# A planner in the kernel orders all operations of attention and two MLPs; joined attention tails, half-bank score tiles, 576-column elementwise work

## The chip, the core and the metric

The kernel runs on one core of one Trainium2 chip. The metric is device time in microseconds. The core has TensorE (PE, matmuls, with PEld for its weight loads), VectorE (DVE), ScalarE (ACT), GpSimd (POOL) and SyncE (SP), which issues the DMA transfers here.

## What is computed

```python
# 4 batches, 8 heads, 576 positions, 64 columns a head
scores = scale * np.matmul(q, k.transpose(0, 1, 3, 2))
mask = (rel >= 0) & (rel < 128)
scores = np.where(mask, scores + bias[None], -1000000000.0)
attn = np.exp(scores - np.max(scores, axis=-1, keepdims=True))
attn = attn / (np.sum(attn, axis=-1, keepdims=True) + 1e-09)
x = np.matmul(attn, v)                       # then (4, 576, 512)
h = np.maximum(x @ w_in, 0.0)                # first MLP, 1024 wide
gate = 1.0 / (1.0 + np.exp(-conv_out))       # conv_out: 3 taps along positions
x = h * gate @ w_out
h = gelu(x @ w2_in); u, v = split(h)         # second MLP
v_n = (v - mu) / np.sqrt(var + 1e-06) * g_ln
v_s = np.einsum('ts,bsd->btd', w_sg, v_n) + b_sg[None, :, None]
out = x + (u * v_s) @ w2_out
```

## The kernel before

Two heads of a batch make a pair, so there are 16 pairs, four a batch. A pair's scores are nine row tiles (qk_rt, L288): for each head four of 128 queries, and one that holds the last 64 queries of both heads. A row tile sees at most 256 keys, since the window is 128. VectorE adds the bias and takes the maximum (sm_max, L323), ScalarE takes the exponential and its sum (sm_exp, L340), TensorE transposes the result (tr1, tr2, L364 and L373) and multiplies it with V.

Precision is kept by splitting a number into a high and a low part that TensorE takes fast: a product is then three fast ones (high by high, high by low, low by high). Pairs 0 to 2 (NAT = 3) take native fp32 scores instead, from 64 rows of a head each. The other 13 pairs split each head (ld_head, hi_head, lo_head, L220 to L262): load, copy of the high part on ScalarE, two differences over 64 rows on VectorE, two transfers that put the parts beside each other. For pairs 0 to 5 the product with V is native fp32 (av, L397); for the other ten it is split too (ev_h, ev_l, av_a), and P is scaled by the reciprocal sums before it is transposed (sm_norm, L355). The last 64 queries of the two heads are four products of 64 columns or rows (L416, L417, or L485, L486).

The first MLP works on half a batch: 290 columns (a column of its neighbour on either side) by eight tiles of 128. For each: 12 products (m1, L593), relu, three taps (m1_c0, m1_c12, L615 and L627), tanh, gate (m1_g2, L635), split (m1_gh, m1_gl). The second product (m2, L649) of one half runs between the first products of the next. Its result goes to DRAM (x2d) and comes back for the second MLP, with V tiles (vt, L771), U tiles (ut, L844), the product with w_sg (m4, L861) and the last product (m5, L897). Weights come as 64-bit numbers and are converted by ScalarE, VectorE and GpSimd (split64, L180).

The order is written by hand. at(t, fn) puts a function in a list under a time t; the list is sorted by t and called, and each engine gets its instructions in that order (with what the framework moves). Times come from constants such as the spacing of the pairs, TP = 10.813 in the first batch. To keep TensorE occupied in the first batch, warm (L531) multiplies the identity by itself, and nothing reads the result: 14 times at first (WM0), once beside each row tile of pairs 0 to 3 (WMP).

```python
    T0 = TP
    for p in range(B * NP):
        T = TP if p < NP else TQ if p < 2 * NP else TS
        att_pair(p, a, T, T0)
        a, T0 = a + T, T
    START = 4 * TP + ST0
```

## Time and profile before

| | us |
|---|---|
| runs (median of 3) | 615.26 (615.2 to 615.96) |
| profiled execution, span of its instructions | 613.6 |
| runs' median above that span | 1.7 |
| PE busy | 591.6 (96%) |
| PEld busy | 546.9 (89%) |
| DVE busy | 467.9 (76%) |
| ACT busy | 384.2 (63%) |
| POOL busy | 183.4 (30%) |

The profile gives its execution's span; no time of its own around the span is given, so the comparison with the runs is by their median. A busy time is the union of the times of an engine's instructions. Matmuls are pipelined: each is shown for some 0.3 us, while the next one starts after 0.1 to 0.2, so a busy TensorE need not be at its full rate, and what a matmul costs is read from the start of the next one.

### The profile page before, as it was taken

What the parts mean: (1) busy time and instruction counts of PE and PEld (TensorE: products, weight loads), DVE (VectorE), ACT (ScalarE), POOL (GpSimd) and SP (SyncE); (2) the same over time, 40 slices, a digit from 0 to 9 for tenths busy, and PEclk for the clock granted to TensorE, in tenths of its full rate; (3) what the DMA queues carried; (4) which work ended last, traced back from release to release, by engine and by line L of the source; (5) the groups of instructions that cost most, each with busy time, mean ns of one, the idle gap of its engine ahead of it and who ended that gap; (6) DMA issues with size and microseconds to landing.
All of it is one profiled execution on the core that took longest, in us unless ns stands there. A gap on an engine that the chain in (4) does not pass through costs nothing.

```text
span 613.6 us, 11909 instructions
## 1 busy us (share of the span) xinstructions
PE 591.6 (96%) x4148; PEld 546.9 (89%) x4148; DVE 467.9 (76%) x1195; ACT 384.2 (63%) x1034; POOL 183.4 (30%) x258
## 2 busy tenths in 40 slices
PE   7999998999999999999999979999999999999997
PEld 5778987888798999999999969988999999999997
DVE  4777899999999999999857899769856547527522
ACT  4566777778787878887756666567545335526320
POOL 3440355543332233323222131621312311131030
PEclk9999998999999999999999989999999999999999
DMA  7443544432333334321004453352222211102132
GB/s 247 167 129 105 168 136 121 110 98 78 96 81 89 104 97 116 90 64 44 21 19 139 150 154 97 112 151 84 67 77 76 81 49 59 50 19 60 40 88 77
DMA packets 43040, 58.44 MB, mean 95 GB/s; under 512 B 6626, under 2 KB 28130, under 8 KB 42980
## 3 DMA queue, kind: packets, MB, share of 16 engines
q1 hardware_dynamic: 42980, 57.69, 32.1%
q8 instruction: 32, 0.52, 0.3%
q14 instruction: 28, 0.23, 0.1%
HBM read 40.56 MB, written 9.44 MB: 81 GB/s over the span
## 4 chain that ended last, share of the span: by engine, by line
PE 69%; DVE 20%; issue 4%; ACT 3%; DMA 3%; POOL 0%; SPq 0%; DVEq 0%; ACTq 0%
PE m2p L664 8%; PE m5p L904 8%; PE m1p L604 8%; PE ups L851 8%; PE vps L778 7%; PE m4p L868 3%; PE m4p L870 3%; PE m4p L869 3%; PE warm L534 3%; DVE c L629 2%; PE S L304 2%; PE A L475 2%; PE S L315 2%; DVE ws L171 2%; DVE c L630 2%
## 5 line engine op out<-in xcount | busy, mean ns | idle before, releaser
L604 PE MATMUL m1p<-x,w 128*128 128x290 f32 x768 | 127.6, 306 | 1.0 <-ACT h L611 1.0
L664 PE MATMUL m2p<-g,wo 128*128 128x288 f32 x768 | 118.8, 299 | 6.0 <-ACT g L104 3.0
L664 PEld LDWEIGHTS m2p<-g,wo 128*128 128x128 f32 x768 | 107.0, 190 | 7.9 <-ACT g L104 3.5
L604 PEld LDWEIGHTS m1p<-x,w 128*128 128x128 f32 x768 | 110.3, 193 | 3.9 <-ACT h L611 1.8
L346 ACT ACTIVATE P<-t,mx 128x256 f32<-128x256 f32 (+1 forms) x144 | 68.0, 473 | 16.5 <-DVE mx L337 8.5
L647 POOL TENSOR_TENSOR g<-c,g 128x288 fp32r<-128x288 f32 x48 | 42.8, 892 | 71.7 <-ACT g L104 70.8
L337 DVE CUSTOM_DVE_ANT_0 t<-S,bias_t 128x256 f32<-128x256 f32 (+1 forms) x128 | 48.2, 380 | 12.2 <-PE S L304 5.8
L904 PE MATMUL m5p<-gg,w 128*128 128x288 f32 x384 | 54.5, 294 | 0.0
L904 PEld LDWEIGHTS m5p<-gg,w 128*128 128x128 f32 x384 | 52.5, 188 | 0.6
L851 PE MATMUL ups<-x,w2h 128*128 128x288 f32 x256 | 51.7, 295 | 0.0
L887 POOL TENSOR_TENSOR gg<-u,gg 128x288 fp32r<-128x288 f32 x32 | 26.0, 815 | 62.8 <-ACT gg L883 62.8
L629 DVE SCALAR_TENSOR_TENSOR c<-h,cw,c 128x288 f32<-128x288 f32 x64 | 36.4, 569 | 10.3 <-ACT c L621 10.3
L633 ACT ACTIVATE c<-c 128x288 f32<-128x288 f32 x64 | 28.2, 441 | 23.7 <-DVE c L630 23.5
L815 POOL TENSOR_TENSOR mv<-mv,mhalf 128x1 f32<-128x1 f32 x18 | 16.2, 900 | 89.3 <-DVE mv L814 89.3
L851 PEld LDWEIGHTS ups<-x,w2h 128*128 128x128 f32 x256 | 41.4, 188 | 0.7 <-DVE u L858 0.2
L315 PE MATMUL S<-qkt 128*128 128x256 f32 x130 | 40.6, 320 | 1.2 <-DVE mx L337 1.1
L778 PE MATMUL vps<-w2h,x 128*128 128x512 f32 x128 | 40.9, 396 | 0.9 <-DVE zv L801 0.6
L883 ACT ACTIVATE gg<-u 128x288 fp32r<-128x288 f32 x32 | 14.1, 443 | 40.4 <-DVE u L877 40.4
L868 PE MATMUL m4p<-ws,vn 128*128 128x288 f32 x128 | 37.9, 296 | 0.0
L851 PE MATMUL ups<-x,w2l 128*128 128x288 f32 x128 | 37.8, 295 | 0.0
L869 PE MATMUL m4p<-ws,vn 128*128 128x288 f32 x128 | 37.7, 294 | 0.0
L870 PE MATMUL m4p<-ws,vn 128*128 128x288 f32 x128 | 37.7, 294 | 0.0
(179 smaller groups left out, 1504.4 us busy)
## 6 DMA issues: line engine op xcount, KB each, us to landing
wr<-in_w_in_dram SPq DMA_DIRECT2D x16, 512.0 KB, 3.8
st<-in_qk_dram SPq DMA_DIRECT2D x26, 288.0 KB, 2.9
qkt<-qkt SPq DMA_DIRECT2D x52, 144.0 KB, 2.4
x2d<-x2o SPq DMA_DIRECT2D x32, 144.0 KB, 2.2
st<-x2d SPq DMA_DIRECT2D x16, 288.0 KB, 2.8
vr<-in_v_dram SPq DMA_DIRECT2D x16, 256.0 KB, 3.0
wr<-in_w_out_dram SPq DMA_DIRECT2D x16, 256.0 KB, 2.7
res<-x2d SPq DMA_DIRECT2D x24, 144.0 KB, 2.1
```

The lines of the kernel that those rows point to most:

```text
L315: pe.matmul(ps, T[:, c:c + 128], T[:, 704 + k0:704 + k0 + 256], start=j == 0, stop=j == n - 1)
L337: dve.tensor_tensor_reduce(t[:, 0:w], src, bs, -0.125, 3e38, ALU.add, ALU.min, mx)
L346: act.activation(P[:, 0:w], t[:, 0:w], AF.Exp, bias=mx[:, i:i + 1], scale=-1.0, accum_out=sm[:, i:i + 1])
L604: pe.matmul(ps, W1[k][w][:, ms], x[:, xi, :], start=n == 0, stop=n == 11)
L629: dve.scalar_tensor_tensor(c, h[:, 1:HS + 1], cw[:, 1, m:m + 1], c, ALU.mult, ALU.add)
L664: pe.matmul(ps, WO[m][:, w, cs], g[:, gi, :], start=(m == 0 and j == 0), stop=(m == 7 and j == 2))
L778: pe.matmul(ps, X[:, xi, k, ts], E[w][:, k, 512:1024], start=j == 0, stop=j == 11)
L851: pe.matmul(ps, E[w][:, k, d * 128:d * 128 + 128], X[:, xi, k, hf * HS:hf * HS + HS], start=j == 0, stop=j == 11)
L868: pe.matmul(ps, vn[:, 0, ds], ws[k][:, 0, cs], start=k == 0, stop=False)
L869: pe.matmul(ps, vn[:, 0, ds], ws[k][:, 1, cs], start=False, stop=False)
L870: pe.matmul(ps, vn[:, 1, ds], ws[k][:, 0, cs], start=False, stop=False)
L904: pe.matmul(ps, E["w3"][k][:, w, c * 128:c * 128 + 128], g[:, gi, :], start=j == 0, stop=j == 11)
```

## The change

The kernel is rewritten. A class Plan takes every operation with its engine, a cost from a formula, a due time t, the data that it reads and writes and the buffers that it needs. run() places them one after the other: on each engine the operation with the earliest due time among those that could start, else the one that could start first, with buffers given out in the order of their first due time. The instructions are then issued in the order so found, and the framework moves none (manual_schedule). Parts of the computation change with it:

- native scores for 4 pairs (NAT = 4), over 128 rows, half of them zeros; 8 pairs with the native product with V and 8 with the split one (APATH) instead of 6 and 10
- a head is split by one difference over 128 rows, and three transfers, each into the place that the one before has read
- the tails of two heads are one 128x128 product (L600, L601; L710, L711)
- four score tiles of 256 columns lie in two PSUM banks; before, two tiles
- in the split pairs the result, not P, is scaled: the reciprocals are spread to 640 columns, transposed and multiplied in
- the MLP's products take 288 columns a half, and its elementwise work (taps, tanh, gate, split) takes both halves at once, 576 columns; all eight m1 tiles of a batch stand ahead of its m2 products by due time
- no warm products

```diff
-NAT, NTM, AM = 3, 7, 'bbbbbbaaaa'
-TP, TQ, TS = 10.813, 10.095, 15.399
...
-WM0, WMP = 14, [1, 1, 1, 1]
+APATH = (7, 9, 10, 11, 12, 13, 14, 15)
...
+NL, LDH, PH, PB0, ALEAD, D0, DS = 28, 15.079, 83.144, 39.047, 10.405, 0.5, 1.939
...
+class Plan:
...
+            for e in ENG:
+                best = None
+                for o in ready[e]:
+                    s = max(free[e], o["r"], free["POOL"] if o["x"] else lock if e == "POOL" else 0.0)
+                    k = (0, o["t"], o["i"]) if s <= free[e] + 1e-6 else (s, o["t"], o["i"])
...
+        for o in order:
+            o["fn"]()
...
+def us_dve(n, ptr=0, fast=0):
+    return (130 + n / 1.92 if fast else 70 + n / 0.96 + 60 * ptr) / 1000
...
+    ctx.enter_context(tc.manual_schedule())
...
+    tag("mm", 2, tiles=bank[0:2])
+    tag("S", 4, tiles=[bank[2 + i // 2][:, 256 * (i % 2):256 * (i % 2) + 256] for i in range(4)])
+    tag("T", 2, tiles=bank[4:6])
...
+    def head(g, t):
...
+        op_copy(HHI, t - LDH + 4, lambda: r(K.ap()), st.ap, (st,), ((K, 0),), S)
+        op_sub(HLO[g % len(HLO)], t - LDH + 4.7, lambda: r(A.ap()[:, 64:640]), st.ap,
+               K.ap, (st, (K, 0)) + ZA, ((A, 0),), S)
+        load(t - LDH + 5.5, lambda: L.ap()[64:128], lambda: A.ap()[64:128, 64:640], ((A, 0),) + ZL, ((L, 0),), 147456)
+        load(t - LDH + 6, lambda: A.ap()[64:128, 64:640], lambda: K.ap()[0:64], ((K, 0), (L, 0)), ((A, 0),), 147456)
+        load(t - LDH + 6.5, lambda: K.ap()[0:64], lambda: K.ap()[64:128], ((A, 0),), ((K, 0),), 147456)
...
+            def tail():
+                o = Bk.ap()[:, 0:128]
+                pe.matmul(o, PT[0, 1].ap()[:, 384:512], vb()[:, 3, :], start=True, stop=False)
+                pe.matmul(o, PT[1, 1].ap()[:, 384:512], vb()[:, 4, :], start=False, stop=True)
...
+        for k in (1, 2):
+            opx("DVE", us_dve(S, 1), t + 0.4 + 0.7 * k, lambda k=k: dve.scalar_tensor_tensor(
+                c.ap(), h.ap()[:, k:k + S], cw[:, k, m:m + 1], c.ap(), ALU.mult, ALU.add), hh + ("cw",), (c,))
```

TensorE at the program's start, before (nat holds the native queries and keys; S is a score tile, T a transpose, warm the product that nothing reads):

```order
L304 MATMUL S<-nat 128x128
L304 MATMUL S<-nat 128x256
L534 MATMUL warm<-ident 128x128 x16
L304 MATMUL S<-nat 128x256
L534 MATMUL warm<-ident 128x128
L368 MATMUL T_238<-ident,P 128x128
L534 MATMUL warm<-ident 128x128
L307 MATMUL S<-nat 64x192
```

And with the change, with the semaphores waited for (ps_74 and ps_75 are the two banks of scores, kn and qn native keys and queries):

```order
L504 MATMUL ps_74<-kn,qn 128x128 [waits DMAHW1_49,DMAHW0_49,DVE_49]
L504 MATMUL ps_74<-kn,qn 128x256
L504 MATMUL ps_75<-kn,qn 128x256 x2
L504 MATMUL ps_74<-kn,qn 128x192 [waits DVE_49]
L504 MATMUL ps_74<-kn,qn 128x192 [waits DMAHW2_49,Pool_49]
L504 MATMUL ps_74<-kn,qn 128x128
L504 MATMUL ps_75<-kn,qn 128x256 [waits DVE_49]
L504 MATMUL ps_75<-kn,qn 128x256
```

The reads of these tiles on VectorE with the change:

```order
L527 ISA t,sm<-ps_74,bias_t 128x128 [waits DVE_49,PE_49]
L527 ISA sm 128x1
L527 ISA t,sm<-ps_74,bias_t 128x256
L527 ISA sm 128x1
L527 ISA t,sm<-ps_75,bias_t 128x256 [waits PE_49]
L527 ISA sm 128x1
L527 ISA t,sm<-ps_75,bias_t 128x256 [waits Activation_49]
```

The warm products are gone, five row tiles stand at the head of the queue, and VectorE waits for TensorE once for each bank, not for each tile.

TensorE in the middle of the first MLP, before (m1p and m2p are results of its first and second products, A of the split product with V):

```order
L604 MATMUL m1p<-x,w_93 128x290 x2
L604 MATMUL m1p<-x,w_94 128x290
L315 MATMUL S<-qkt 128x256
L317 MATMUL S<-kl,qkt 128x256
L315 MATMUL S<-qkt 128x256
L317 MATMUL S<-kl,qkt 128x256
L664 MATMUL m2p<-g,wo_99 128x288 x3
L664 MATMUL m2p<-g,wo_100 128x288 x3
```

And with the change, at the end of the first batch's first products (ps_72 and ps_73 are the two banks of the MLP; L778 is the first product, L808 the second, L509 a split score, L565 a transpose, L590 a product with V):

```order
L778 MATMUL ps_73<-x,w_766 128x288 x12
L626 MATMUL ps_79<-ident_80,xt 128x128
L778 MATMUL ps_72<-x,w_842 128x288 x12
L778 MATMUL ps_73<-x,w_842 128x288 x12
L808 MATMUL ps_72<-g,wo 128x288 x12
L565 MATMUL ps_76<-ident_80,P 128x128 x4
L808 MATMUL ps_73<-g,wo 128x288 x6
L590 MATMUL ps_78<-v_98,pt 128x64 x3
L808 MATMUL ps_73<-g,wo 128x288 x6
L509 MATMUL ps_75<-kh,qa_94 128x192
```

First and second products no longer alternate: the last first product is followed at once by the second products, and the attention's pieces stand between runs of six or twelve.

SP's queue in the first MLP batch with the change (kl, qa and kh are the three operands of a head, raw is a weight, v a load of V; before, a head had two such transfers, qkt<-qkt):

```order
L319 DMA kl_96<-qa_94 64x576 [waits DMAHW2_49,PE_49]
L319 DMA raw<-in_w_out_dram 128x1024 [waits DMAHW3_49]
L319 DMA qa_94<-kh 64x576 [waits DMAHW4_49,DMAHW2_49]
L319 DMA kh<-kh 64x576 [waits DMAHW5_49,DMAHW4_49]
L319 DMA raw<-in_w_out_dram 128x1024 [waits DMAHW6_49,DVE_49]
L319 DMA v_99<-in_v_dram 128x4x128 [waits DMAHW7_49,PE_49]
```

A transfer of a head now waits in SP for the landing of the head's transfer before it, with weight and V loads behind it.

## Rows read from the trace of the kernel before

**Rows 1.** By stage: us; busy PE, PEld, DVE, ACT, POOL; clock; DMA share; GB/s.
```profile
0.00:59.70 59.70, 55.39 (x347) 42.84 (x347) 40.22 (x131) 35.47 (x108) 20.03 (x41) 1.00 0.50 162
59.70:225.00 165.30, 156.67 (x1133) 141.40 (x1132) 156.83 (x440) 129.69 (x390) 64.81 (x94) 0.99 0.39 108
225.00:330.00 105.00, 104.99 (x800) 100.46 (x799) 86.68 (x242) 79.75 (x236) 31.16 (x50) 1.00 0.23 65
330.00:401.70 71.70, 67.33 (x469) 65.39 (x468) 62.54 (x112) 45.60 (x102) 21.31 (x20) 0.98 0.44 133
401.70:613.60 211.90, 207.23 (x1408) 196.79 (x1407) 121.65 (x273) 93.64 (x201) 46.09 (x53) 1.00 0.23 68
```

**Rows 2.** Timeline of TensorE: start, us, instruction; first matmuls and first MLP product.
```profile
4.31 1.62 PE L304 MATMUL S<-nat 64*128 64x128 f32 x4 [4.31 <-DMA nat<-in_qk_n_dram]
5.86 6.23 PE L534 MATMUL warm<-ident 128*128 128x128 f32 x32
...
59.68 0.38 PE L604 MATMUL m1p<-x,w 128*128 128x290 f32 x1
```

**Rows 3.** Chain of waits, two runs of 12 MLP products.
```profile
212.26 1.63 PE m1p L604 x12
...
220.35 1.60 PE m2p L664 x12
```

**Rows 4.** Timeline of TensorE: native score, product with V, transpose, split score.
```profile
20.49 0.70 PE L304 MATMUL S<-nat 64*128 64x256 f32 x2
21.11 0.32 PE L408 MATMUL O<-vr,pt 128*128 128x64 f32 x1
...
31.24 0.27 PE L368 MATMUL T<-ident,P 128*128 128x128 f32 x1
31.35 0.27 PE L369 MATMUL T<-ident,P 128*128 128x128 f32 x1
...
37.13 0.39 PE L407 MATMUL O<-vr,pt 128*128 128x64 f32 x2
37.35 0.39 PE L408 MATMUL O<-vr,pt 128*128 128x64 f32 x2
...
58.95 0.28 PE L317 MATMUL S<-kl,qkt 128*128 128x256 f32 x1
59.07 0.28 PE L315 MATMUL S<-qkt 128*128 128x256 f32 x1
```

**Rows 5.** Groups by line and shape, VectorE and ScalarE: busy us, mean ns.
```profile
L337 DVE CUSTOM_DVE_ANT_0 t<-S,bias_t 128x256 f32<-128x256 f32 x96 | 39.2, 413 | 8.8 <-PE S L304 4.9 <-ACT P L346 1.6 <-PE S L317 1.3
...
L261 DVE TENSOR_TENSOR kl<-st,qkt 64x576 fp32r<-64x576 f32 x26 | 23.0, 886 | 0.8
...
L260 DVE TENSOR_TENSOR qkt<-st,qkt 64x576 fp32r<-64x576 f32 x26 | 19.5, 750 | 0.0
L104 ACT ACTIVATE qkt<-st 128x576 fp32r<-128x576 f32 x26 | 17.7, 680 | 1.3 <-PE S L315 0.7 <-PE S L317 0.6
...
L358 DVE TENSOR_SCALAR P<-P,rc 128x256 f32<-128x256 f32 x40 | 16.3, 439 | 0.0
...
L791 DVE SCALAR_TENSOR_TENSOR zu<-zu,ups 128x288 f32<-128x288 f32 x32 | 14.2, 449 | 5.6 <-ACT zu L787 5.5
...
L142 DVE TENSOR_TENSOR x<-st,x 128x576 fp32r<-128x576 f32 x16 | 13.9, 871 | 3.4 <-ACT x L104 3.3
...
L791 DVE SCALAR_TENSOR_TENSOR zv<-zv,vps 128x512 f32<-128x512 f32 x18 | 12.3, 684 | 10.6 <-ACT zv L787 10.4
```

**Rows 6.** Busy time as in rows 1, five us of the last MLP batch.
```profile
360.00:365.00 5.00, 3.45 (x15) 3.34 (x15) 4.97 (x8) 2.69 (x6) 1.54 (x2) 0.68 0.36 110
```

**Rows 7.** DMA issues: KB each, median us from issue to landing.
```profile
st<-in_qk_dram SPq DMA_DIRECT2D x26, 288.0 KB, 2.9
...
qkt<-qkt SPq DMA_DIRECT2D x52, 144.0 KB, 2.4
...
nat<-in_qk_n_dram SPq DMA_DIRECT2D x4, 288.0 KB, 5.1
```

More of the change, by code (lines that the diff above doesn't have):

```diff
@@ L102, in copy, with r, new @@
[L102 to L113 removed]
+    def r(ap):
+        return ap.bitcast(F32R)
+    def new(tag, n, name):
+        return Buf(plan, tag, n, name)
@@ new lines @@
+    A1 = ("A", "KL", "V") + tuple(x for x, _ in ATAGS)
+    for name, count in PTAGS:
+        tag(name, count, "p2", need=A1)
+    tag("zv", 3, tiles=h_t, need=("h",))
+    tag("u", 4, tiles=c_t + fixed(main, "u", 1, S), need=("c",))
+    tag("v", 3, tiles=bank[2:5], need=("S", "T"))
+    tag("u2", 3, tiles=bank[5:8], need=("T", "O", "B"))
+    W2 = {(k, hf): new("W", 1024, "w2") for k in range(4) for hf in range(2)}
+    WS = [new("L", 1152, "ws") for _ in range(5)]
+    W3 = [new("L", 1024, "w3") for _ in range(4)]
@@ L1070 @@
+    plan.run()
 def kernel(**inputs):
```

1699 lines of the change are left out of this document (840 added, 859 removed).

## The prediction

> **What bounds the kernel now.** I read the busy times by stage first, because a share over the whole span is an average. The stages are cut at the first MLP matmul (59.7 us), where the attention work thins out (225, 330), and at the end of the first MLP (401.7) [rows 1]. The reader should compare matmuls per microsecond, since TensorE's busy time is the union of overlapping matmuls and counts their latency. From 225 to 330 us TensorE is never idle and takes 800 matmuls in 105.0 us, 0.131 us each, with VectorE busy for 86.7 us (83%). From 59.7 to 225 us the same mixture of attention and MLP takes 165.3 us for 1133 matmuls, 0.146 us each; there VectorE is busy for 156.8 us (95%) and TensorE idle for 8.6. So this stretch is VectorE's. From 330 to 401.7 TensorE is idle for 4.4 us, again with VectorE near full. The last stage, 211.9 us, has TensorE busy for 207.2.
>
> The first 59.7 us are nobody's: VectorE 40.2, ScalarE 35.5, and of TensorE's passes 100 are the warm product, which nothing reads. The first matmul waits 4.31 us for its load, the 32 warm passes behind it take 6.23 us, 0.195 us each, and the first MLP product comes at 59.68 [rows 2]. What spaces the pairs there is the order written out by hand: TP puts them 10.813 apart.
>
> **Part A, up to the first MLP product.** The new order puts before it 40 instructions of native scores (24 of 256 columns, 8 of 128, 8 of 192), 79 transposes, 52 products with V, 6 tail products and 14 split score products. A transpose follows the next after 0.11 us, a split score product after 0.12, a product with V (two passes) after 0.22 [rows 4]. A native score instruction over 64 rows took 0.62 us for its two passes [rows 4]; the change gives it 128 rows, half of them zeros, and the trace has no such instruction. The warm passes give a lower price: 0.195 us for 128 columns of 128 rows [rows 2], nearly twice a transpose of as many columns, so I read them as run at 1.2 GHz (an inference from the durations), and at 2.4 they are about 0.1, 0.2 for 256 columns, 0.4 for the two passes. I take 0.4, because the warm product has the same 128 rows and the same type; the upper end is 0.62. By columns, the native scores are 24 x 0.4 + 8 x 0.2 + 8 x 0.3 = 13.6 us (21 at the upper end). The rest is 79 x 0.11 + 52 x 0.22 + 6 x 0.22 + 14 x 0.12 = 23.1. Together 36.7 us.
>
> The start: 4.31 us now, with loads of 144 KB. The new order waits for a load of 288 KB, which took 5.1 us from its issue [rows 7]; with about a microsecond until it is issued, 4.3 to 6.4, and I take 5.5. Warm-up: by that reading 32 passes took 6.2 us instead of about 3.1; without the warm product real matmuls bear the same loss, 3.1. Waits among the engines have no row for this order. Below they are 0; above, the stage is as long as now, 59.7. I take 5, near the low end, because neither VectorE nor ScalarE was over 67% busy there. The sum is 5.5 + 36.7 + 3.1 + 5 = 50.3, so A is **-9.4** (-14 to 0).
>
> **Part B, from there to the last product of the first MLP.** Removed passes. The MLP goes from 290 to 288 columns: 12 products took 1.63 and 1.60 us [rows 3], 768 x 0.03/12 = 1.9 us less; I take 1.3, since other runs of 12 are closer. Attention, with the prices above: before, 246 split scores (29.5), 224 transposes (24.6), 42 products with V (9.2), 120 + 20 products of the second path (14.4 + 4.4), and the 64-wide pieces of the tails, 60 at about 0.22 (13.2): 95.3. Now 226 split scores (27.1), 257 transposes, those of the reciprocals among them (28.3), 60 products with V and 26 tails (18.9), 128 of the second path (15.4): 89.7. That is -5.6, together **-7**.
>
> VectorE. From 59.7 to 330 it is busy for 243.5 of 270.3 us. Three things leave it. Joining two halves of 288 columns: 288 columns took 449 ns and 512 took 684 [rows 5], so 1.05 ns a column and 147 ns an instruction; three instructions for each of 24 tiles in this stretch save 24 x 3 x 0.147 = 10.6 us. Splitting a head in one instruction over 128 rows: 886 + 750 ns for each of 26 heads become one like the 871 of x [rows 5] for each of 24, 42.5 - 20.9 = 21.6 us, about 19 in this stretch. The scaling of P leaves (16.3 us for the 256-column pieces alone), and 8 pairs get one multiply of 512 columns (0.68) and two small ones (0.2): -7.7. Together -37 us: 206 of some 245 us, 84%, which is the share at which TensorE was never idle. ScalarE is late next: 209.5 of 270.3 us now, and as the scaling's spreading (640 columns a pair) gives back about what its joined halves save, some 85%. GpSimd takes all low parts, 32 instructions of 576 columns in place of 48 of 288; it is busy for 96 of 270 us, and that covers them.
>
> So the rate of 0.131 should hold: 1133 x (0.146 - 0.131) = 17 us. I take 15, leaving 2 to the new order's own waits (ends: 0 and 17), and half of the 4.4 idle us of the last MLP batch, 2 (ends 0 and 4.4), since VectorE still splits the second MLP's weights there. B is -7 - 15 - 2 = **-24**.
>
> **Part C, the rest.** The same 1408 matmuls; TensorE has 4.7 idle us. I take **-1** (-2 to +4).
>
> **Sum.** 613.6 - 9.4 - 24 - 1 = 579.2 for the profiled execution's span. The runs' median, 615.26, is 1.7 above that span, which I carry over: **580.9 us**. A difference under 0.2% (1.2 us) is about what a measurement of this kernel can't tell from none.
>
> **A rule against the change.** Two score tiles now share a bank. The listing with its waits shows what that does: of four reads in a row VectorE waits for TensorE at the first of each bank only, so it waits until both halves are written, and TensorE in turn waits before it writes a half. The Trainium skill (PSUM, PSUM bank collisions raise a hardware error) says the same: engines are to be kept apart by bank and quadrant, not by address. No run here shows what it costs; by the rule four half banks are two buffers, as before, and the time is that of rival 1, 590.
>
> **Rivals.** (1) The shared banks bind. A read takes 413 ns [rows 5]. If TensorE stands still for one read at each second half, that is 18 x 0.41 = 7 us in the first stage, and 72 x 0.41 = 30 if it happens in all. Against it: between scores the later order has runs of 6 to 12 MLP products (0.8 to 1.6 us), in which reads finish. Time 588 to 611, I say 590; chance 0.12.
>
> (2) The waits stay: another order of the same dependences loses as much, because an order fixed by a list of costs can't yield to late transfers. Then B keeps only its 7 us of passes and A half of its gain: 613.6 - 4.7 - 7 + 1.7 = **604**. For it: the old order was fixed beforehand too, and had its waits. Against it: the stretch lost its time where VectorE was full, and that work leaves. Chance 0.18.
>
> (3) Slower: SP. A head now needs its load (2.9 us), its copy and difference [rows 5], and three transfers of 2.4 each [rows 7], each behind the landing of the one before, for the halves are overwritten in place: 2.9 + 0.68 + 0.87 + 7.2 = 11.7 of the 15.08 that LDH gives. SP stands at such a transfer, and behind it wait V loads, weight loads and stores of x2d. From 3.4 us of lateness a head on, every further microsecond holds TensorE 24 times; at 5 us late that is 24 x 1.6 = 38 us, which takes back the whole gain: **619**. Against it: SP's three transfers block it for 7 us per head, 24 x 7 = 173 of some 245 us, so it has room, if little. Chance 0.07.
>
> (4) The clock stays low in the first stage, now that nothing fills TensorE's gaps. From 360 to 365 us, with TensorE busy for 3.45 of 5 us, the mean granted clock was 0.68 of 2.4 GHz, so part of the stretch ran at 1.2 [rows 6]; at 1.2 GHz throughout, A's 36.7 us double: 580.9 + 36.7 - 3.1 = **614.5**, no difference. Against it: native scores alone occupy it well. Chance 0.03.
>
> That the order does not move at all is excluded by the listings.
>
> **How the numbers follow.** My forecast, 581 us, has 0.60. Its own range comes from A (-14 to -4), B (-7 to -28) and C (-2 to +1): 571 to 605, most of it under 592. The low end, with nearly every wait gone, is 613.6 - 14 - 28 - 2 + 1.7 = 571; below it lies only a first stage with cheaper native scores, so I put 565. The upper end takes in (2) and most of (1), 605, and leaves out (3), (4) and their neighbours. Faster: 0.60 + 0.11 + 0.17 = 0.88; same: 0.03; slower: 0.07 and 0.02 from the upper ends of (1) and (2), 0.09.
>
> **What would show it.** Right: the first MLP product near 50 us; from there to the last about 318 us, with 0.131 us a matmul and VectorE near 84%; 211 us behind it. Rival 1: in the first stage TensorE's idle time put down to VectorE's reads of scores. Rival 2: VectorE or ScalarE full again in the middle. Rival 3: score products waiting for transfers. Rival 4: a granted clock near half before 50 us. The forecast is wrong if the middle stretch keeps 0.146 us a matmul.

## The result, and the profile after

The changed kernel takes **599.3 us** (median of 596.7 to 600.7), the kernel before beside it 615.2: a ratio of 0.973 (0.970 to 0.976). It is faster, by 16 us; I had forecast 34. The time lies in my range and the sign is right, but 16 of the 34 us came.

By stage (us; busy PE, PEld, DVE, ACT, POOL; clock; DMA share; GB/s), cut at the same events as [rows 1]:

```profile
0.00:56.50 56.50, 43.78 (x290) 38.70 (x290) 38.71 (x154) 41.36 (x124) 26.67 (x34) 1.00 0.67 186
56.50:225.00 168.50, 160.16 (x1251) 157.07 (x1251) 130.20 (x317) 137.18 (x354) 38.22 (x25) 0.99 0.44 121
225.00:310.00 85.00, 83.88 (x653) 81.77 (x652) 59.24 (x157) 67.15 (x180) 17.39 (x12) 1.00 0.29 74
310.00:388.60 78.60, 67.70 (x458) 63.92 (x458) 61.41 (x78) 46.84 (x86) 27.33 (x18) 0.96 0.39 122
388.60:596.80 208.20, 203.27 (x1397) 194.88 (x1396) 117.05 (x264) 96.92 (x206) 50.93 (x61) 1.00 0.23 70
```

The first MLP product comes at 56.5 us, 3.2 earlier than before (forecast 9.4). From there to the last product of the first MLP it takes 332.1 us, 9.9 less (forecast 24). Behind it 208.2, 3.7 less (forecast 1). From 225 to 310 a matmul takes 0.130 us, as hoped; from 56.5 to 225 it takes 168.5/1251 = 0.135, although VectorE is busy for only 77% there; and in the last MLP batch, 310 to 388.6, TensorE idles for 10.9 us where before it idled for 4.4.

The 77% is itself an average over two different parts:

```profile
56.50:130.00 73.50, 66.44 (x509) 64.21 (x509) 66.06 (x147) 62.12 (x157) 22.68 (x14) 0.98 0.50 139
130.00:225.00 95.00, 93.72 (x744) 92.86 (x743) 64.14 (x170) 75.06 (x198) 15.54 (x11) 1.00 0.39 107
```

All of the lost time lies before 130 us, where VectorE is busy for 66.1 of 73.5 us and a matmul takes 0.144 us; behind it the share is 68% and a matmul takes 0.128.

TensorE's longest waits (us in total, times, longest):

```profile
PE ps L940 <- ACT x L292: 6.0, 1, 6.0
PE ps L504 <- DMA qn<-in_qk_n_dram: 5.4, 1, 5.4
PE ps L565 <- ACT P L534: 3.5, 2, 3.3
PE ps L504 <- DVE sm L527: 3.4, 5, 1.4
PE ps L808 <- ACT h L784: 2.7, 3, 1.3
PE ps L509 <- DVE sm L527: 2.0, 2, 1.4
```

The first lies in the last MLP batch, the second at the program's start. What makes operations late is seen on VectorE and GpSimd in the last MLP batch. Two timelines (start, us, instruction), VectorE and then GpSimd:

```profile
333.20 0.81 DVE L791 SCALAR_TENSOR_TENSOR c<-h,cw,c 128x576 f32<-128x576 f32 x1
333.93 1.96 DVE L794 SCALAR_TENSOR_TENSOR c<-c,h 128x576 f32<-128x576 f32 x1
335.81 1.85 DVE L791 SCALAR_TENSOR_TENSOR c<-h,cw,c 128x576 f32<-128x576 f32 x1
337.59 1.63 DVE L397 TENSOR_SCALAR gs<-gs 128x512 int32<-128x512 int32 x1
339.14 0.74 DVE L794 SCALAR_TENSOR_TENSOR c<-c,h 128x576 f32<-128x576 f32 x1
```

```profile
333.37 1.90 POOL L313 TENSOR_TENSOR g<-c,g 128x576 fp32r<-128x576 f32 x1 [4.04 <-ACT g L292]
335.24 1.81 POOL L313 TENSOR_TENSOR w<-gs,w 128x512 fp32r<-128x512 f32 x1
336.99 1.94 POOL L313 TENSOR_TENSOR g<-c,g 128x576 fp32r<-128x576 f32 x1
```

L791 takes 0.81 us where it starts ahead of GpSimd's operation and 1.85 where GpSimd started first; L794 takes 0.74 with GpSimd idle and 1.96 beside it. The three long ones end 0.6, 0.6 and 0.3 us behind GpSimd's ends (335.27, 337.05, 338.93). For each form of a VectorE instruction (line, operation, shapes) I take the duration a fifth of the way up from the fastest, and call an instruction stretched when it takes over 60 ns more than that; the excess is its stretch. In this trace 43 of 967 are stretched, by 31.8 us together, 11.8 of it between 320 and 360 us. All 43 overlap a GpSimd instruction; of all 967 only 303 do.

### The profile page after: what moved, and what is told of

The parts are those of the page before. It is cut to its first block, busy times and chain, and to the rows that moved or that the text cites. A ratio compares the mean times of both kernels' runs of the same rounds, so it can differ in the third digit from the quotient of the medians.

```text
span 596.8 us, 11161 instructions
## 1 busy us (share of the span) xinstructions
PE 558.8 (94%) x4040; PEld 536.3 (90%) x4040; DVE 406.6 (68%) x967; ACT 389.5 (65%) x948; POOL 160.5 (27%) x150
## 4 chain that ended last, share of the span: by engine, by line
PE 58%; DVE 21%; ACT 11%; DMA 4%; issue 3%; SPq 1%; POOL 0%; DVEq 0%; ACTq 0%
PE ps L808 12%; PE ps L940 8%; PE ps L988 7%; PE ps L1042 7%; DVE c L791 6%; PE ps L778 5%; PE ps L1009 3%; PE ps L1011 3%; PE ps L1010 3%; ACT P L534 2%; PE ps L509 2%; PE ps L565 2%; DVE c L794 2%; DVE gs L407 2%; PE ps L504 2%
## 5 line engine op out<-in xcount | busy, mean ns | idle before, releaser
L778 PE MATMUL ps<-x,w 128*128 128x288 f32 x768 | 115.6, 299 | 1.9 <-ACT h L784 1.7
L808 PE MATMUL ps<-g,wo 128*128 128x288 f32 x768 | 113.7, 299 | 3.3 <-ACT h L784 2.7
L808 PEld LDWEIGHTS ps<-g,wo 128*128 128x128 f32 x768 | 104.7, 189 | 4.8 <-ACT h L784 3.3
L778 PEld LDWEIGHTS ps<-x,w 128*128 128x128 f32 x768 | 104.3, 188 | 2.9 <-ACT h L784 2.9
L313 POOL TENSOR_TENSOR g<-c,g 128x576 fp32r<-128x576 f32 x32 | 50.9, 1592 | 138.7 <-ACT g L292 103.6
L534 ACT ACTIVATE P<-t,sm 128x256 f32<-128x256 f32 (+1 forms) x144 | 67.7, 472 | 13.0 <-DVE sm L527 12.6
L527 DVE CUSTOM_DVE_ANT_0 t<-ps,bias_t 128x256 f32<-128x256 f32 (+1 forms) x128 | 46.9, 384 | 24.4 <-PE ps L509 14.4
L791 DVE SCALAR_TENSOR_TENSOR c<-h,cw,c 128x576 f32<-128x576 f32 x64 | 59.5, 932 | 3.2 <-ACT c L788 2.6
L988 PE MATMUL ps<-x,w 128*128 128x288 f32 x384 | 54.1, 295 | 1.1 <-DVE c L998 1.1
L1042 PE MATMUL ps<-gg,w 128*128 128x288 f32 x384 | 54.6, 294 | 0.0
L988 PEld LDWEIGHTS ps<-x,w 128*128 128x128 f32 x384 | 52.2, 188 | 1.7 <-DVE c L998 1.3
L1042 PEld LDWEIGHTS ps<-gg,w 128*128 128x128 f32 x384 | 52.6, 188 | 0.7
L313 POOL TENSOR_TENSOR w<-gs,w 128x512 fp32r<-128x512 f32 x20 | 27.9, 1401 | 60.5 <-ACT w L292 56.8
L565 PE MATMUL ps<-ident,P 128*128 128x128 f32 x256 | 39.0, 276 | 4.8 <-ACT P L534 3.5
L1009 PE MATMUL ps<-ws,vn 128*128 128x288 f32 x128 | 37.8, 295 | 0.0
L1011 PE MATMUL ps<-ws,vn 128*128 128x288 f32 x128 | 37.7, 295 | 0.0
L1010 PE MATMUL ps<-ws,vn 128*128 128x288 f32 x128 | 37.6, 294 | 0.0
L565 PEld LDWEIGHTS ps<-ident,P 128*128 128x128 f32 x256 | 30.8, 143 | 6.7 <-ACT P L534 4.6
L509 PE MATMUL ps<-kh,qa 128*128 128x128 f32 (+2 forms) x120 | 33.3, 296 | 2.2 <-DVE sm L527 2.0
```

Of the source, the lines that this page charges most:

```text
L313: op(e, cost, t, lambda: engines[e].tensor_tensor(o(), a(), b(), ALU.subtract), R, W, x=x and e == "DVE")
L534: act.activation(P[rt].ap()[:, 0:w], tt.ap()[:, 0:w], AF.Exp, bias=sm.ap()[:, c:c + 1], scale=-1.0, accum_out=sm.ap()[:, 9 + c:10 + c])
L565: pe.transpose(ps.ap()[:, 128 * j:128 * j + 128], x.ap()[:, c:c + 128], ident)
L778: pe.matmul(ps.ap()[:, 0:HS], w1(m)[:, w, k, :], x[:, xi, :], start=k == 0 and j == 0, stop=k == 3 and j == 2)
L791: opx("DVE", us_dve(S, 1), t + 0.4 + 0.7 * k, lambda k=k: dve.scalar_tensor_tensor(c.ap(), h.ap()[:, k:k + S], cw[:, k, m:m + 1], c.ap(), ...
L808: pe.matmul(ps.ap()[:, 0:HS], wo(m)[:, w, 128 * c:128 * c + 128], g[:, gi, :], start=m == 0 and j == 0, stop=m == 7 and j == 2)
```

## The experiments

The table has the median of the runs, and from the profiled execution the start of the first MLP product and of the last second product, the time from the last batch's first product to that last second product, and the stretch of VectorE so counted.

| kernel | us | first | last | last batch | stretch |
|---|---|---|---|---|---|
| changed | 599.3 | 56.5 | 388.4 | 73.7 | 31.8 |
| s0_own | 599.6 | 57.4 | 389.6 | 73.7 | 31.0 |
| banks_alt | 604.6 | 59.6 | 396.2 | 75.0 | 32.2 |
| bias_late | 597.3 | 53.3 | 386.4 | 73.7 | 30.6 |
| bias_warm | 599.0 | 52.4 | 388.1 | 74.7 | 31.7 |
| bias_sign | 598.8 | 52.5 | 389.1 | 74.9 | 30.8 |
| w1_skip | 596.8 | 50.2 | 383.2 | 73.6 | 27.9 |
| half576 | 609.7 | 54.2 | 397.7 | 76.3 | 37.9 |
| nolow | 589.2 | 56.3 | 378.3 | 68.7 | 14.5 |
| low_scratch | 601.7 | 55.8 | 389.5 | 74.8 | 31.4 |
| low3_dve | 596.5 | 56.4 | 387.1 | 69.9 | 23.8 |
| best1 | 595.0 | 53.1 | 383.2 | 69.8 | 13.3 |
| best2 | 595.9 | 53.6 | 383.6 | 68.2 | 8.1 |
| w2_skip | 597.1 | 56.5 | 384.9 | 70.1 | 27.3 |
| nolow_w2skip | 587.7 | 54.7 | 374.8 | 67.8 | 13.1 |
| replan | 576.5 | 47.5 | 366.5 | 59.4 | 2.1 |
| replan_low_gp | 586.8 | 46.8 | 375.7 | 63.9 | 25.6 |
| replan_gp | 602.4 | 52.8 | 391.9 | 74.9 | 37.0 |

The ratios to the kernel before have 95% intervals of some 0.003 to either side, 2 us; kernels nearer than that are not told apart by their time, only by their stages. The stages vary too: changed, half576, nolow, low_scratch, low3_dve, w2_skip and nolow_w2skip have the same instructions in the same order up to the first MLP product, and it comes at 54.2 to 56.5 us; bias_late, best1 and best2 share theirs too, and it comes at 53.1 to 53.6. A new plan changes the whole order, so in all runs but replan and replan_gp the plan is made as in the kernel that they start from, and only what an operation does, its engine, its tile or (late tables) its place is exchanged when it is issued.

**Do the shared banks cost the first stage anything?** s0_own:

```diff
-                self.tile = t["tiles"][self.slot][:, 0:self.n]
+                self.tile = t["own" if getattr(self, "own", 0) else "tiles"][self.slot][:, 0:self.n]
...
-    tag("T", 2, tiles=bank[4:6])
+    tag("T", 2, tiles=bank[4:6]); plan.tags["S"]["own"] = [bank[2], bank[3], bank[0], bank[1]]
...
-            ps = new("S", 256, "S")
+            ps = new("S", 256, "S"); ps.own = nat
```

> The planned order is kept word for word; only the score tiles of the four native pairs (first stage) get whole banks of their own, two of them the MLP product's banks, which nothing uses until 56 us. In the changed kernel TensorE waits 3.4 us in the first stage for score reductions (L527), and the list of waits has one wait for each pair of half-bank tiles, so a tile waits for its neighbour's reduction too. Theory 'shared banks': those 3.4 us go, the first MLP product comes at 53 to 54 instead of 56.5, and the kernel is 2.5 to 3.5 us faster. Theory 'VectorE and the loads pace the first stage': the waits move to another name, the first MLP product stays within 1 us of 56.5, the kernel within 1 us.

599.6 us, first product at 57.4; the waits on L527 were 2.9 us instead of 3.4. With every tile in a bank of its own nothing is won in the kernel's time. For the stage by itself the run settles less, because the granted clock of TensorE was low in two parts of it (the columns of the stages), where the changed kernel's first stage had 1.00:

```profile
25.00:30.00 5.00, 4.45 (x24) 4.33 (x25) 3.15 (x10) 2.12 (x6) 1.04 (x2) 0.66 1.01 255
...
50.00:57.40 7.40, 7.40 (x42) 7.40 (x41) 4.73 (x19) 5.32 (x16) 4.10 (x3) 0.56 0.43 129
```

A mean of 0.56 is the lower level, 1.2 GHz, for some 6.5 of the 7.4 us; in the 5 us ahead of them TensorE was busy for 3.2. My estimate from this row is that at the upper level the stretch would have been some 3 us shorter and the first product near 54, at the early end of what the changed kernel's own order gives. At 45 us TensorE had begun 223 matmuls here and 216 in the changed kernel. So a gain of up to 2 us in this stage is not excluded. The next run changes who shares with whom, in all stages:

```diff
-    tag("S", 4, tiles=[bank[2 + i // 2][:, 256 * (i % 2):256 * (i % 2) + 256] for i in range(4)])
+    tag("S", 4, tiles=[bank[2 + i % 2][:, 256 * (i // 2):256 * (i // 2) + 256] for i in range(4)])
```

> Same order; only which half of which bank a score tile lies in: tiles that follow one another lie in different banks now, and the first shares its bank with the third. Theory 'shared banks': the pairing decides when TensorE may write, so the waits on L527 change in every attention stage and the time moves by 1 to 4 us, for the better if a neighbour's reduction was what was waited for, for the worse if the third tile now waits for the first. Theory 'sharing costs nothing': all waits and the time as before within 0.7 us.

604.6 us, ratio 0.982 (0.979 to 0.985): 5.3 us slower. In the profiled execution the first product is 3.1 us later, of which up to 1.7 can be a granted clock of 0.66 between 30 and 35 us. So the pairing is felt when it is chosen badly; as the change has it, no cost shows in the kernel's time.

**What holds the first stage?** The trace shows the head of VectorE's queue, in the changed kernel:

```profile
6.39 0.76 DVE L351 TENSOR_SCALAR bias_t<-rel 128x256 bf16<-128x256 f32 x1
...
7.08 2.49 DVE L351 TENSOR_SCALAR bias_t<-rel 128x256 bf16<-128x256 f32 x7
9.49 0.28 DVE L527 CUSTOM_DVE_ANT_0 t<-ps,bias_t 128x128 f32<-128x128 f32 x1
```

All eight bias tables stand before the first score reduction, which needs one of them. bias_late:

```diff
+def later(order):
+    late = [o for o in order if o["e"] == "DVE" and o["c"] == 0.27 and o["t"] >= -40]; order = [o for o in order if o not in late]; mx = [o for o in order if o["fn"].__name__ == "mx"]
+    [order.insert(order.index(mx[2 + j]) + 1, o) for j, o in enumerate(late)]; return order
...
-        self.span = max(o["end"] for o in order)
+        self.span = max(o["end"] for o in order); order = later(order)
```

> Same order, except that six of the eight bias-table products on VectorE (L351, eight of them take 3.1 us from 6.4 to 9.5 while the first four score tiles lie ready) go one by one behind the third to eighth score reduction. Theory 'head of VectorE's queue': the first score reduction comes at about 7.7 instead of 9.5, the first MLP product at 54.5 to 55, the kernel 1.5 to 2 us faster. Theory 'shared banks' or 'loads': what is saved at the head is lost again within the first 20 us, the first MLP product moves by under 0.5 us.

The first reduction came at 7.37. The first MLP product, in TensorE's timeline (start, us, instruction):

```profile
53.35 1.03 PE L778 MATMUL ps<-x,w 128*128 128x288 f32 x6
```

The stage is 3.1 us shorter than in the changed kernel's trace, where 2.1 were moved at its head; against the seven executions with the old tables it is 1 to 3 us. Of it the kernel kept 2.0 us (597.3), about what the intervals can tell.

On top of it, three runs: products that nothing reads before the first score, the sign step of the W1 conversions on VectorE, and the W1 conversions without their bit work.

```diff
-        dve.memset(mhalf, -0.5)
+        dve.memset(mhalf, -0.5); [pe.transpose(bank[7][:, 0:128], ident, ident) for _ in range(14)]
```

> The kernel with the late bias tables (597.3 us, first MLP product at 53.3), and 14 transposes of the identity on TensorE from about 1.5 us, before the first score tile; nothing reads them. In the kernel without them the first eight passes of the first score tiles take 3.3 us, at 5.4 to 8.8, and from 10 us on a pass of 256 columns takes 0.22. Theory 'cold TensorE at the start': the first passes take half as long, the first reduction comes 0.5 to 1 us earlier, and the first MLP product 1 to 2 us earlier. Theory 'VectorE and the loads pace the start': under 0.5 us.

First MLP product at 52.4, 0.9 us earlier, which is hardly clear of the spread; the kernel at 599.0 shows nothing of it.

```diff
-            if e1 == "DVE":
+            if e1 == "DVE" or eng is CV0:
```

> The kernel with the late bias tables, and the sign step of the eight W1 conversions on VectorE (0.42 us each) instead of GpSimd (2.0 us each, where the planner reckons 0.2 + 1.2 x 0.512 = 0.81 us), at the same places. Theory 'mis-priced GpSimd step': the W1 chain (sign, or, bits, high, low) is 1.6 us shorter per slice and VectorE is not stretched; first MLP product 1 to 2 us before 53.3. Theory 'W1 is ready in time anyway': the first MLP product within 0.5 us of 53.3, or later by up to 1 us for 3.4 us more VectorE work.

52.5, 0.8 us earlier, hardly clear of the spread either, and 598.8: no gain for the kernel.

```diff
-        op(e1, us_copy(e1, n), t + 0.6, sign, ((s2, "g"),), ((s2, "s"),))
...
+        skip = key in W1; op(e1, us_copy(e1, n), t + 0.6, (lambda: None) if skip else sign, ((s2, "g"),), ((s2, "s"),))
...
-        opx("DVE", us_dve(n), t + 1.6, bits, ((s2, "s"),), ((s2, "g"),))
+        opx("DVE", us_dve(n), t + 1.6, (lambda: None) if skip else bits, ((s2, "s"),), ((s2, "g"),))
```

> The kernel with late bias tables (597.3; first MLP product at 53.3), less the bit work of the eight W1 conversions (sign on GpSimd 8 x 2.0, two steps on VectorE 8 x 1.2 us), so the values differ. Theory 'contention paces the first stage': the first MLP product comes 2 to 4 us before 53.3. Theory 'the chain of an attention pair (score, reduction, exponential, transposes, product, normalising) and TensorE's own passes pace it': within 1 us of 53.3.

The first MLP product in TensorE's timeline:

```profile
50.18 1.03 PE L778 MATMUL ps<-x,w 128*128 128x288 f32 x6
```

3.2 us earlier than with the late tables alone, and no wait of TensorE in the first stage of either kernel names a tile of W1: the weight conversions compete with the attention there. Late tables and conversions together are 6.3 us, which is all that the first stage lacked of the forecast (50.3). The kernel's time is not measurably better (596.8).

**Do the wide operations carry the gain?** half576 issues the taps, the gate and tanh in halves, the first tap and tanh on ScalarE among them; the diff shows the taps on VectorE:

```diff
-            opx("DVE", us_dve(S, 1), t + 0.4 + 0.7 * k, lambda k=k: dve.scalar_tensor_tensor(
-                c.ap(), h.ap()[:, k:k + S], cw[:, k, m:m + 1], c.ap(), ALU.mult, ALU.add), hh + ("cw",), (c,))
+            opx("DVE", us_dve(S, 1), t + 0.4 + 0.7 * k, lambda k=k: [dve.scalar_tensor_tensor(
+                c.ap()[:, i:i + HS], h.ap()[:, k + i:k + i + HS], cw[:, k, m:m + 1], c.ap()[:, i:i + HS], ALU.mult, ALU.add) for i in (0, HS)], hh + ("cw",), (c,))
```

> Undoes the 576-column part alone, in the changed kernel's order: the two taps and the gate on VectorE, and the first tap and tanh on ScalarE, as two instructions of 288 columns each at the same places (96 more on VectorE, 64 more on ScalarE). On VectorE 288 columns of such a form cost about 0.43 us each by the ones with 288 in this trace (L998, L1049) and 576 cost 0.81, with a start-to-start distance about 0.07 under the duration, so 96 x 0.06 = 6 us more work. Theory 'the wide operations carry much of the gain': 602 to 606. Theory 'VectorE is not the bound any more': within 1.5 us of 599.3.

609.7 us, 10 more, beyond what either theory gave. In this order, which was planned for them, the wide operations are worth about 10 of the 16 us.

**GpSimd's operations themselves, or the wait for their result?** nolow leaves the low parts of g out:

```diff
-        op_sub(e[1], t + 4.7, lambda: r(g.ap()[:, S:2 * S]), c.ap, lambda: g.ap()[:, 0:S], (c, (g, 0)), ((g, 1),), S)
+        op(e[1], us_pool(S, 1), t + 4.7, lambda: None, (c, (g, 0)), ((g, 1),))
...
-                for j, (w, gi) in enumerate(((0, 0), (0, 1), (1, 0))):
+                for j, (w, gi) in enumerate(((0, 0), (0, 0), (1, 0))):
```

> Leaves out the 32 low parts of g (128x576 on GpSimd, 1.6 us each, 51 us in all); the second MLP product uses the high part in their place, with as many TensorE passes, so its values differ. All other instructions and their order are kept. So this takes away GpSimd's traffic beside VectorE in the MLP batches and nothing else. Theory 'collisions': of 32.5 us by which VectorE operations were stretched, under 15 stay; the last MLP product ends at 380 to 384 instead of 388.5, and the kernel takes 591 to 595 instead of 599.3. Theory 'amount of VectorE and ScalarE work, or other waits': the stretches go, but the time stays within 2 us, since VectorE waits instead.

589.2 us, ratio 0.958 (0.957 to 0.960): 10 us, all of them between the first and the last MLP product. The stretch falls to 14.5. From 56.3 to 225 us a matmul takes 0.131 us now:

```profile
56.30:225.00 168.70, 163.67 (x1287) 161.45 (x1287) 126.58 (x324) 138.92 (x360) 14.49 (x10) 0.99 0.46 124
```

low_scratch takes the second half of that diff alone: GpSimd makes the low parts and nobody reads them.

> GpSimd still makes the 32 low parts of g at the same places, but nobody reads them: the second MLP product uses the high part in their place, as in the run without the low parts (589.2 us), so its values differ. GpSimd's traffic beside VectorE stays, only TensorE's waits for the low parts go. Theory 'collisions': 597 to 600, stretches near 32 us, since the traffic is what costs. Theory 'the low part comes late for the second product': 589 to 592.

601.7 us with a stretch of 31.4. With GpSimd's operations there and no reader of their result nothing is won, so the 10 us are the price of these operations beside the others and not of waiting for what they make. In the list of all waits of low_scratch no engine waits for a low part of g either, which speaks against a buffer that GpSimd gives back late. VectorE's tap and GpSimd's low part in the groups by line (count, busy us, mean ns, idle before), of low_scratch:

```profile
L791 DVE SCALAR_TENSOR_TENSOR c<-h,cw,c 128x576 f32<-128x576 f32 x64 | 59.3, 929 | 3.2 <-ACT c L788 2.8
...
L313 POOL TENSOR_TENSOR g<-c,g 128x576 fp32r<-128x576 f32 x32 | 50.0, 1564 | 139.5 <-ACT g L292 109.2 <-PE ps L590 15.3 <-PE ps L509 9.3
```

and of nolow:

```profile
L791 DVE SCALAR_TENSOR_TENSOR c<-h,cw,c 128x576 f32<-128x576 f32 x64 | 56.0, 876 | 3.9 <-ACT c L788 3.4
```

**Can VectorE do the low parts itself?** In the last batch (low3_dve, whose diff stands below), in all (best1, with the late tables), and the low parts of W2 as well (best2):

```diff
-    def op_sub(e, t, o, a, b, R, W, n, x=1):
+    def op_sub(e, t, o, a, b, R, W, n, x=1, on=None):
-        op(e, cost, t, lambda: engines[e].tensor_tensor(o(), a(), b(), ALU.subtract), R, W, x=x and e == "DVE")
+        op(e, cost, t, lambda: engines[on or e].tensor_tensor(o(), a(), b(), ALU.subtract), R, W, x=x and e == "DVE")
...
-        op_sub(e[1], t + 4.7, lambda: r(g.ap()[:, S:2 * S]), c.ap, lambda: g.ap()[:, 0:S], (c, (g, 0)), ((g, 1),), S)
+        op_sub(e[1], t + 4.7, lambda: r(g.ap()[:, S:2 * S]), c.ap, lambda: g.ap()[:, 0:S], (c, (g, 0)), ((g, 1),), S, 1, "DVE" if b == 3 else None)
```

> Same order; only the eight low parts (128x576) of the last MLP batch run on VectorE at the places that the plan had for them on GpSimd. VectorE gains 8 x 0.75 = 6 us of work, GpSimd loses 8 x 1.6 us, and with it some of the 8 us or so by which VectorE operations are stretched beside GpSimd between 320 and 360 us. Theory 'collisions of VectorE and GpSimd': the stretch goes, the last MLP product ends 2 to 4 us earlier than 388.6, the kernel is 2 to 4 us faster. Theory 'too much VectorE work in the last MLP batch, whoever collides': the stage gets 2 to 5 us longer.

> Late bias tables, and all 32 low parts of g on VectorE (0.75 us each, 24 us more for it) at the places that the plan had for them on GpSimd, nothing left out. Leaving them out altogether gave 589.2, leaving eight of them to VectorE in the last batch 596.5, the late bias tables 597.3. Theory 'collisions': GpSimd's low parts cost more than they carry, and VectorE (68% busy) has room: 590 to 594. Theory 'the low parts cost by their place in a chain, whoever runs them, or VectorE gets full': 597 or more.

> As the one before, and the low parts of the eight W2 conversions on VectorE too (8 x 0.68 us), so that GpSimd is idle beside the last MLP batch. Theory 'collisions': the stretches between 320 and 370 us go, 0.5 to 2 us faster than the one before. Theory 'VectorE is the bound of the last batch': 1 to 4 us slower than it.

596.5, 595.0 and 595.9 us. From the first product of the last batch to its last second product low3_dve took 69.9 us instead of 73.7, with 6 us more work on VectorE. best1 is 2.3 us faster than the late tables alone, at the edge of what the intervals tell and a miss of the 590 to 594 expected. Its gain lies in the last batch (69.8 us instead of 73.7); from the first MLP product to that batch it takes 260.3 us, the kernel with the late tables 259.4. The 24 us of low parts cost VectorE little more when it makes them (busy for 409.2 us in all) than when GpSimd does (405.7 in bias_late). In best2 the W2 parts gain nothing more. All three keep an order planned for GpSimd's share; whether that limits them is asked below.

**Is VectorE's work in the last batch the rest?** w2_skip leaves out the bit work of the W2 conversions (the diff of w1_skip with W2.values() for W1), nolow_w2skip the low parts of g too.

> Leaves out the bit work on VectorE (L397, L402, L407: 8 x 1.6 = 13 us) of the eight W2 conversions, which run between 310 and 365 beside the last MLP batch; the second block's values differ. Everything else and the order are kept. Theory 'too much VectorE work in the last MLP batch': VectorE paces TensorE there; the stretch from the last batch's first product to the last second product gets 6 to 10 us shorter, the kernel 592 or less. Theory 'collisions alone': 2 to 4 us, because fewer operations are hit. Theory 'chain of h, tanh and g per tile': under 1 us.

> Leaves out both the low parts of g (589.2 us alone) and the bit work of the W2 conversions (597.1 alone, against 599.3). With the low parts left out, TensorE still idles 6.8 us between 310 and 380. Theory 'VectorE's amount of work paces the last batch once collisions are gone': those 6.8 us fall to 3 or less, the kernel takes 585 or less. Theory 'the chain of a tile (first product, h, two taps, tanh, gate, copy) or the reload of x paces it': 587 to 589.

597.1 and 587.7 us: 2.2 and 1.5 less than with the conversions, hardly more than the error. The last batch is shorter by 3.5 us beside GpSimd's low parts (70.1 instead of 73.7) and by 0.9 without them (67.8 instead of 68.7), and in nolow_w2skip TensorE still idles for 5.0 us between 310 and 376 us. So the amount of VectorE's work counts in the last batch beside GpSimd's low parts, but it is not what is left when they are gone.

**With an order planned for a quiet GpSimd.** replan has the late tables, the low parts of g and all conversion steps that were GpSimd's on VectorE, and tells the planner so; start times and spacings are then set anew by the plan's own end.

```diff
-GHE = (("ACT", "POOL"), ("ACT", "DVE"))
+GHE = (("ACT", "DVE"), ("ACT", "POOL"))
...
-CV0 = ("ACT", "POOL", "ACT", "POOL")
+CV0 = ("ACT", "DVE", "ACT", "DVE")
...
-CV2 = ("ACT", "DVE", "ACT", "POOL")
+CV2 = ("ACT", "DVE", "ACT", "DVE")
...
-NL, LDH, PH, PB0, ALEAD, D0, DS = 28, 15.079, 83.144, 39.047, 10.405, 0.5, 1.939
...
+NL, LDH, PH, PB0, ALEAD, D0, DS = 28, 15.911, 83.328, 38.716, 11.68, 0.357, 1.881
...
-WO0, WO1, LCW, W20, W21, X20, WS0 = 41.21, 5.577, 6.871, -19.494, 4.55, -2.265, 7.237
...
+WO0, WO1, LCW, W20, W21, X20, WS0 = 44.604, 5.446, 6.871, -19.115, 4.216, -26.924, 5.87
```

> Late bias tables; all low parts of g and all steps of the W1 and W2 conversions but the scaling and the high part on VectorE, so GpSimd is quiet in the first stage and beside the MLP batches; the planner is told so and its numbers (start times and spacings of the stages) are set anew. By its order the first MLP product comes 4 us earlier than in the kernel with the late tables alone, and the last MLP batch is shorter. Theory 'collisions and the order planned without them': what is planned is kept, the first MLP product at 48 to 50, the whole 584 to 590. Theory 'any such plan loses some 20 us on the chip by waits that it does not see': 592 or more.

**576.5 us**, ratio 0.936 (0.934 to 0.938), better than either theory: 23 us below the changed kernel and 39 below the one before. By stage and in its first waits:

```profile
0.00:47.00 47.00, 40.74 (x285) 37.12 (x285) 38.23 (x158) 39.29 (x122) 7.37 (x23) 1.00 0.80 212
47.00:225.00 178.00, 170.34 (x1300) 165.80 (x1299) 139.50 (x356) 142.53 (x366) 6.52 (x5) 0.97 0.44 121
225.00:310.00 85.00, 84.61 (x667) 83.76 (x666) 62.04 (x160) 68.25 (x177) 3.94 (x3) 1.00 0.31 84
310.00:370.00 60.00, 60.00 (x419) 57.96 (x419) 54.22 (x92) 42.37 (x80) 0.58 (x1) 1.00 0.43 142
370.00:576.00 206.00, 199.86 (x1378) 191.84 (x1376) 117.15 (x266) 96.46 (x206) 48.95 (x58) 0.99 0.23 69
```

```profile
PE ps L504 <- DMA qn<-in_qk_n_dram: 5.4, 1, 5.4
PE ps L565 <- ACT P L534: 3.6, 4, 1.5
PE ps L778 <- ACT h L784: 1.2, 2, 1.0
```

From 310 to 370 us TensorE never idles, while VectorE is busy for 54.2 of 60 us: its share there is higher than in the changed kernel (61.4 of 78.6), and TensorE waits less. The gain stands at both ends: the first MLP product is 9.0 us earlier than in the changed kernel, and the last batch 14.2 us shorter (59.4 instead of 73.7). Between the first MLP product and the last batch nothing is won (259.6 us, the changed kernel 258.3). There a matmul takes 178/1300 = 0.137 us from 47 to 225, and VectorE still fills up, with GpSimd idle beside it:

```profile
97.00:107.00 10.00, 7.63 (x49) 6.06 (x48) 10.00 (x23) 7.97 (x19) 0.00 (x0) 1.00 0.14 30
```

Two runs part the order from GpSimd's share. replan_low_gp gives the low parts back to GpSimd in this very order:

```diff
-        op_sub(e[1], t + 4.7, lambda: r(g.ap()[:, S:2 * S]), c.ap, lambda: g.ap()[:, 0:S], (c, (g, 0)), ((g, 1),), S)
+        op_sub(e[1], t + 4.7, lambda: r(g.ap()[:, S:2 * S]), c.ap, lambda: g.ap()[:, 0:S], (c, (g, 0)), ((g, 1),), S, 1, "POOL")
```

> The order of the re-planned kernel (576.5 us) word for word, but the 32 low parts of g run on GpSimd again, at the places that they had on VectorE. VectorE has 24 us less to do, GpSimd 51 us more; the W1 and W2 conversions stay on VectorE. Theory 'GpSimd's traffic costs VectorE more than its work is worth': stretches of 15 us or more come back, and the time is 579 to 586. Theory 'the new order, not the quiet GpSimd, is the gain': within 1.5 us of 576.5, or faster.

586.8 us: 10.3 slower with 24 us less work on VectorE, whose other instructions are stretched by 25.6 us instead of 2.1. On the pages of the two runs VectorE is busy for 411.1 us with the low parts and for 415.2 without them. Some of the 10.3 us is another cost: in this run, unlike in the changed kernel, TensorE waits for the low parts themselves, 2.7 us in three waits. The tap of the one and of the other in the groups by line, replan first:

```profile
L791 DVE SCALAR_TENSOR_TENSOR c<-h,cw,c 128x576 f32<-128x576 f32 x64 | 52.0, 813 | 2.1 <-ACT c L788 1.9
...
L313 DVE TENSOR_TENSOR g<-c,g 128x576 fp32r<-128x576 f32 x32 | 24.1, 753 | 0.6 <-ACT g L292 0.4
```

```profile
L791 DVE SCALAR_TENSOR_TENSOR c<-h,cw,c 128x576 f32<-128x576 f32 x64 | 62.4, 975 | 2.7 <-ACT c L788 2.3
```

replan_gp has new numbers found in the same way, and GpSimd's share as in the change:

```diff
-NL, LDH, PH, PB0, ALEAD, D0, DS = 28, 15.079, 83.144, 39.047, 10.405, 0.5, 1.939
...
+NL, LDH, PH, PB0, ALEAD, D0, DS = 28, 13.738, 83.144, 38.65, 10.634, 0.5, 1.939
```

> A control: the same kind of new numbers for the planner, found in the same way, with the same late bias tables, but with the low parts of g and the steps of the weight conversions on GpSimd as in the changed kernel. Theory 'collisions': whatever the numbers, GpSimd's share of the work costs its 10 us or more: 590 to 598. Theory 'the changed kernel's numbers were merely poor': 576 to 583.

602.4 us, no better than the changed kernel: this one set of new numbers gains nothing while GpSimd has its share.

## Why the prediction was right in sign and wrong in size

**Part A** said -9.4, with the first MLP product at 50.3; it came at 56.5. The start was right (first score at 5.43, forecast 5.5), and so was the taken price of a 256-column native tile: 0.43 us in a row of the changed kernel, forecast 0.4 (TensorE's timeline, from one start to the next).

```profile
29.90 0.60 PE L504 MATMUL ps<-kn,qn 128*128 128x256 f32 x2
30.33 1.00 PE L590 MATMUL ps<-v,pt 128*128 128x64 f32 x8
```

The step that failed is the 5 us of waits. It weighed the shares of VectorE and ScalarE (67% at most) and overlooked what stands ahead in the queue: the tables and the W1 conversions' steps. They measured 3.1 and 3.2 us, and without both the product came at 50.2. That this is the forecast's number is in part luck: replan makes all the conversions and comes at 47.5. TensorE's idle time behind the start was 7.3 us, 2.3 more than the 5; the other 4 of the 6.2 us that A missed stand in its busy time (43.8 us, where 36.7 and 3.1 were forecast), and in it a pause shorter than the time for which a matmul is shown does not appear. The 3.1 us taken for the warm-up have one run beside them, bias_warm, and it gave 0.9; and the reading behind them, that the warm passes ran at 1.2 GHz, has the granted clock of that stage against it, which is 1.00 in [rows 1].

**Part B** said -24 and measured -9.9; here is the main error. The removed work was right: VectorE's busy time from the first MLP product to 310 us is 189 of 253.5 us, 75%, even below the 84% forecast, and half576 shows that the wide operations matter. The step that failed is the inference behind "the rate of 0.131 should hold" and the 2 us for the last batch: that VectorE at 84% leaves TensorE without idle time, and that GpSimd "covers" the low parts because it is free for more than half of the time. A GpSimd operation of 1.6 us is not beside VectorE's work but in its way. And 84% was an average over 270 us: as the two rows of the middle stage show, VectorE is full in one part and half free in the other. That GpSimd is in the way I could have read in two places. In the trace of before, by the same count, 101 VectorE instructions are stretched by 43.3 us, all of them while GpSimd runs, 21.9 us of it between 59.7 and 225; the 95% of [rows 1] were partly waiting. And in the diff the planner's own line lets a marked VectorE operation start only when GpSimd is free; the program contains no wait for that, so on the chip the operations meet when either is late.

The terms, measured by counting what a stage takes above 0.131 us a matmul: from the first MLP product to 225 us this fell from 16.9 to 4.6 us, so the rate gave 12.3 of its 15, and the 4 to 5 us that are left are what nolow wins there (it has 0.131). In the last MLP batch (330 to 401.7 before, 310 to 388.6 now) it rose from 10.3 to 18.6, so the -2 became +8.3: this term is the larger part of the miss, and TensorE's idle time there rose by 6.5 instead of falling by 2. The 40 matmuls fewer are 5.2 us, where 7 was taken for the passes. From its first product to its last second product the last batch takes 73.7 us, and 68.7 without GpSimd's low parts. The rest is the order there, as far as the trace shows it: one wait of 6.0 us for the split of x, which nolow has too (5.4), and a granted clock of 0.66 on average beside it, as in [rows 6] of before. The busy times of these ten us, in the columns of the stages:

```profile
350.00:360.00 10.00, 4.85 (x14) 3.63 (x15) 9.97 (x11) 6.82 (x11) 5.21 (x3) 0.66 0.24 82
```

VectorE is full, TensorE half idle; in this batch replan has neither the wait nor the low clock and takes 59.4 us.

In replan, with GpSimd quiet, the first MLP takes 319 us (47.5 to 366.5), where the forecast had 318. That is in part luck and does not confirm the sum: by the same count replan loses 7.7 us from 47 to 225, where the forecast left 2, and 5.1 from 310 to 370, where it left some 8, and VectorE does work there that the forecast had on GpSimd.

**Part C** said -1 and measured -3.7, outside its bounds (-2 to +4) on the good side. TensorE's idle time is as forecast, 4.9 us. Its stage has 1397 matmuls instead of 1408, because more of the second MLP's first products stand ahead of the cut (37 instead of 25); at 0.131 us that is 1.6 us, and no run parts the rest.

**The rule weighed** (the Trainium skill, PSUM — Partial Sum Buffer, PSUM bank collisions raise a hardware error) and **rival 1** put 7 us on the first stage. s0_own shows none of it in the kernel's time and leaves some 2 us open in the stage. The pairwise waits exist, and banks_alt shows 5.3 us for the worse pairing. **Rival 2**, 604, is nearest in time and in its parts (A -4.7 and B -7, measured -3.2 and -9.9): waits remained, but its reason, that any fixed order loses as much, falls with replan. **Rival 3**: no wait of TensorE for the transfer of a head is among the waits of the changed kernel's trace. **Rival 4**: the clock in the first stage is 1.00.

The rule that I should have weighed stands on another page. The Trainium skill (SBUF — State Buffer, SBUF: two separate sides) says that a VectorE operation with two SBUF inputs and a GpSimd operation that reads SBUF share one port pair: the one that starts first has it for its whole instruction, and the other waits. The trace agrees: the two-operand L794 above, which started 0.56 us behind GpSimd's operation, ended 0.62 us behind its end, and takes 0.74 us alone.

What stays open: replan_low_gp, with the low parts on GpSimd, is at 586.8 us still 8 below best1, which has them on VectorE. These 8 us come from the conversions on VectorE and the new numbers together; the runs don't part them, and only exclude the numbers by themselves (replan_gp). Open is too why the 0.8 to 3 us won in the first stage didn't reach the end in bias_warm, bias_sign and w1_skip.
